# Columns beside the keys: zeros by a bf16 matmul, filled by GpSimd in SBUF from the fourth pair of heads on

## The chip, the cores and the metric

The kernel runs on one core of a Trainium2 chip. The metric is device microseconds of one execution. TensorE is PE in the rows (its weight loads PEld), VectorE is DVE, ScalarE is ACT, GpSimd is POOL, and SP is the queue that issues most of the DMAs.

## What is computed

Chunked attention with memory keys feeds a top-1 mixture of experts. The change lies in the attention, which is, cut to what matters:

```
B, H, S, D = 4, 8, 768, 64;  chunk, left, right, n_mem = 32, 16, 8, 8
for c in range(S // chunk):
    ctx = [max(0, 32*c - 16), min(S, 32*c + 40))
    k_full = concat(mem_k, k[ctx]);  v_full = concat(mem_v, v[ctx])
    scores = q[chunk c] @ k_full.T / sqrt(D)
    a = softmax(scores)                  # with the row's maximum taken off
    out[chunk c] = a @ v_full
x = out as [3072, 512];  e = argmax(x @ w_gate + bias);  y = gate * relu(x @ w1[e]) @ w2[e]
```

Chunk 0 has no 16 keys to its left, and chunk 23 no 8 keys to its right.

## The kernel before

The 32 heads are worked in 16 pairs, u = 0 to 15, and each pair in two halves of 12 chunks (hf = 0 and 1). I write S0(u) and S1(u) for the scores of the two halves. Every chunk has 64 key columns in the tile `kbd` (two buffers, by u % 2): 56 keys of the sequence and 8 memory keys. The two heads of a pair stand in the two halves of the partitions.

- `trans_k(u+1)` (L337), in the first half of pair u, transposes the keys of each head on PE into one PSUM bank (three transposes, L343). The bank has 8 columns to the left and 8 to the right of the keys, which the windows of chunks 0 and 23 reach into. A matmul in float32 fills these 16 columns with memory keys (L347), so that they never raise a row's maximum; the rows of V that belong to them are zero.
- `store_k` (L349) copies the windows from PSUM to `kbd`, four copies on ACT (L353).
- `mem_keys(u+2)` (L332) writes the 8 memory columns of every chunk, two copies on POOL (L335), one pair ahead.
- `share_v(u+1)` (L304), eight copies on POOL (L311), repeats the 24 rows of V that two chunks share. The first waits for V to land from DRAM. In the second half of pair u it stands on POOL ahead of `mem_keys(u+2)`, and behind both comes the store of the outputs of an earlier pair (L418).
- `exps_t` transposes scores (L379) and takes the exponential on ACT (L381, tile PT); `attend` multiplies by V (L391); `trans_x` transposes the output (L413), ACT copies it (L416).
- `route(b)` finds the experts of a batch of four pairs. Its steps are dealt out among those of the attention by `pump`. Where two of its one-hot pairs go to POOL (L663, L665), they stand behind L606 and L418 and ahead of the next `share_v`: this is so ahead of pairs 8, 12 and 15.

PE, SP and POOL run in the order in which the program is written, ACT and DVE too until pair 13. In the loop below, an iteration is one half of a pair: scores, exponentials of the half before, then in the first half `trans_k`, `store_k`, in the second `share_v`, `mem_keys`, `trans_q`, then `attend` of the half before.

Of the kernel before, what the change touches and what calls it, by code (L numbers as in the profile page):

```python
# [20 lines left out]
P = 128  # L21
B, H, S, D = 4, 8, 768, 64
NMEM = 8
NCH = S // 32
# [7 lines left out]
NTAIL = 8  # L32
NEXTRA = 7
HEAD = 3
LAST = 3
ROW_R1 = HEAD + NTAIL + 1
ROW_X = ROW_R1 + 1
# [15 lines left out]
def tile_chunk_attention_top1_moe(  # L53
# [14 lines left out]
    nc = tc.nc  # L68
# [24 lines left out]
    def bank():  # L93
        return ps.tile([P, 512], F32, name="tr", tag="tr", bufs=4)
# [14 lines left out]
    idle = const.tile([P, 640], BF16, name="idle")  # L109
# [16 lines left out]
    kbds = [pers.tile([P, NCH, 2, 64], F32, name=f"kbd{i}") for i in range(2)]  # L126
# [12 lines left out]
    mkp = pers.tile([P, P], F32, name="mkp")  # L139
# [9 lines left out]
    ident = const.tile([P, P], F32, name="ident")  # L149
# [19 lines left out]
    memT = pers.tile([P, 16, NMEM], F32, name="memT")  # L169
# [15 lines left out]
    listed, turn0, ends, tail_no, at_r1, at_x = (rows[:, i:i + 1] for i in range(6))  # L185
# [15 lines left out]
    def more_constants():  # L201
# [30 lines left out]
        yield "v"  # L232
        nc.vector.tensor_scalar(tail_no, row, HEAD - 0.5, None, op0=ALU.is_gt)
        yield "v"
# [3 lines left out]
        yield "v"  # L238
        nc.vector.scalar_tensor_tensor(turn0, turn0, float(HEAD - ROW_X), row, op0=ALU.mult, op1=ALU.add)
        yield "v"  # L240
        nc.vector.scalar_tensor_tensor(turn0, ends, float(ROW_X - HEAD + 2 - ROW_L - LAST), turn0, op0=ALU.mult, op1=ALU.add)
        yield "v"
        nc.vector.tensor_scalar(turn0, turn0, -2.0, None, op0=ALU.add)
        yield "v"
        nc.vector.tensor_scalar(tail_no, row, HEAD + NTAIL + 0.5, float(1 - 64), op0=ALU.is_gt, op1=ALU.mult)
        yield "v"
        nc.vector.tensor_add(tail_no, tail_no, row)
        yield "v"
        nc.vector.tensor_scalar(tail_no, tail_no, float(-HEAD), None, op0=ALU.add)
        yield "v"  # L250
# [53 lines left out]
    def share_v(u):  # L304

        vw = vws[u % NVW]
        for h in range(2):
            r0 = 64 * h
            for c in range(0, NCH - 1, 6):
                w = min(6, NCH - 1 - c)  # L310
                nc.gpsimd.tensor_copy(vw[r0:r0 + 24, h, c + 1:c + 1 + w, 0:D], vw[r0 + 32:r0 + 56, h, c:c + w, 0:D])  # L311

    def regroup_q(u):
        q2 = q2s.pop(u)
        qr = qrs[u] = wk.tile([P, 6, 2, D], F32, name="qr", bufs=1)
        nc.vector.tensor_copy(
            qr.rearrange("p x h d -> p h x d"), q2.rearrange("p h (x d) -> p h x d", d=D)
        )
# [18 lines left out]
    def trans_k(u):  # L337
        k2 = k2s.pop(u)
        for h in (1, 0):
            hh = 2 * u + h  # L340
            t = kts[u, h] = bank()
            for i in range(3):
                nc.tensor.transpose(t[:, 8 + i:8 + i + 382:3], k2[:, h, i * P:(i + 1) * P], ident)  # L343

            pads = bass.AP(tensor=t.tensor, offset=t.offset, ap=[list(t.ap[0]), [392, 2], [1, 8]])
            mem_sel = ident[:, 4 * hh:4 * hh + 4].unsqueeze(1).unsqueeze(1)
            nc.tensor.matmul(pads, mkp, mem_sel.to_broadcast([P, 2, 2, 4]), start=True, stop=True)  # L347

    def store_k(u, h, j, copy):  # L349
        tt = kts[u, h][64 * j:64 * j + 64]  # L350
        win = bass.AP(tensor=tt.tensor, offset=tt.offset, ap=[list(tt.ap[0]), [16, NCH], [1, 28]])
        dst = kbds[u % 2][64 * h:64 * h + 64, :, h, 0:56]
        copy(dst.rearrange("p c (i j) -> p c i j", j=2)[:, :, :, j], win)  # L353

    def scores(u, hf):
        kbd, qT = kbds[u % 2], qTs[u]
        sc = scs[u, hf] = ps.tile([P, 512], F32, name="sc", tag="sc", bufs=2)
        for t in range(3):
            for j in range(4):
                c = 4 * (3 * hf + t) + j  # L360
                nc.tensor.matmul(  # L361
                    sc[32 * j:32 * j + 32, t * P:(t + 1) * P], qT[:, 32 * c:32 * c + 32],
                    kbd[:, c].rearrange("p h m -> p (h m)"), start=True, stop=True,
                )

    def less_max(u, hf):
        scf = scs.pop((u, hf))[:, 0:384].rearrange("p (a m) -> p a m", m=64)
        mx = sm.tile([P, 6, 1], F32, name="mx")
        nc.vector.reduce_max(mx, scf, axis=AX.X)
        pump(1)  # L370
        sb = sbs[u, hf] = wk.tile([P, 6, 64], F32, name="sb")
        nc.vector.tensor_sub(sb, scf, mx.to_broadcast([P, 6, 64]))

    def exps_t(u, hf):

        sb = sbs.pop((u, hf)).rearrange("p a m -> p (a m)")
        t = bank()
        for i in range(3):
            nc.tensor.transpose(t[:, i * P:(i + 1) * P], sb[:, i * P:(i + 1) * P], ident)  # L379
        PT = PTs[u, hf] = wk.tile([P, 3 * P], F32, name="PT")  # L380
        nc.scalar.activation(PT, t[:, 0:384], AF.Exp, scale=scale)  # L381
# [82 lines left out]
    def plan_rest():  # L464
# [39 lines left out]
        vec.tensor_scalar(turn, ends, end[:, E - 1:E], turn0, op0=ALU.mult, op1=ALU.add)  # L504
        vec.tensor_scalar(nsl[:, 0:1], end[0:1, E - 1:E], float(2 - HEAD - LAST), None, op0=ALU.add)
        vec.tensor_mul(sta, sta, noth)
# [373 lines left out]
    nc.gpsimd.memset(vws[1][64:P, 0], 0.0)  # L880
    edge_v(1)
    trans_k(0)
    t = bank()
    nc.tensor.transpose(t[:, 0:P], mk, ident)
# [22 lines left out]
    for i in range(n + 2):  # L907
        live = i < n
        u, hf = units[i] if live else (NU, i % 2)
        now[0] = i  # L910
        if i == MAN:
            man.close()
        if live and i < n - 1:
            scores(u, hf)
        if 1 <= i <= n:
            exps_t(*units[i - 1])
        if live:
            less_max(u, hf)
            pump(1)
        if u + 1 < NU and hf == 0:  # L920
            trans_k(u + 1)
            regroup_q(u + 1)
            pump(3)
            store_k(u + 1, 1, 0, nc.scalar.copy)
            store_k(u + 1, 0, 0, nc.scalar.copy)
            store_k(u + 1, 0, 1, nc.scalar.copy)
            store_k(u + 1, 1, 1, nc.scalar.copy)
            pump(3)
        elif u + 1 < NU:
            share_v(u + 1)  # L930
            if u + 2 < NU:
                mem_keys(u + 2, nc.gpsimd)
            trans_q(u + 1)
            store_q(u + 1, 0)
            store_q(u + 1, 1)
            pump(5)
        elif live:
            pump(5)
        first = i in (n - 3, n - 2)
        if first:  # L940
            trans_x(*units[i - 2])
        if i == n - 2:
            scores(*units[i + 1])
        if 1 <= i <= n:
            attend(*units[i - 1])
        if i == n:
            trans_x(*units[i - 2])
            trans(0)
            trans(1)
            conv(4)  # L950
            conv(5, nc.gpsimd)
            normalize(*units[i - 1])
            mm1(0)
        if i > n:
            mm1(1)
        if i >= 2 and not first and i != n:
            trans_x(*units[i - 2])
        if 1 <= i < n:
            normalize(*units[i - 1])
            pump(1)  # L960
        if i >= 2:
            u2, hf2 = units[i - 2]
            if hf2 == 1 and u2 % 4 == 3:
                routing.append((route(u2 // 4), True, u2 // 4, 0))
        if i == 1:
            routing.append((more_constants(), False, -1, 0))
        if i == 6:
            assert not routing
            bias_rows()
        if i < n:  # L970
            pump(1, True)
        if live and hf == 0:
            if u + 3 < NU:
                load_qk(u + 3)
            if u >= 1 and u - 1 + NVW < NU:
                load_v(u - 1 + NVW)
        if (u, hf) == (NU - 2, 1):
            while routing:
                pump(99, True)
            c_ld.close()  # L980
            xp = ctx.enter_context(tc.tile_pool(name="xp", bufs=1, side="right"))
            ix = xp.tile([P, 2], I32, name="ix")
            gx = xp.tile([P, 2], I32, name="gx")
            xg = [xp.tile([P, XW], F32, name=f"xg{t}") for t in range(2)]
            xth, xtl = [xp.tile([P, 4, 256 + NR], F32R, name=f"xt{i}") for i in range(2)]
            hh, hl = [xp.tile([P, 8, 256], F32R, name=f"h{i}") for i in range(2)]
            load_w(0, 0)
            gather(0)
        elif u == NU - 1:
            conv(2 * hf)  # L990
            conv(2 * hf + 1, nc.gpsimd)
# [137 lines left out]
    more.close()  # L1129
    for i in range(1, LAST + 1):  # L1130
        slot(ROW_L + i if i < LAST else None)

# [29 lines left out]
```

## Time and profile before

| what | value |
|---|---|
| three runs | 442.55, 445.7, 446.6 us, median 445.7 |
| the profiled execution | 444.6 us, span 442.8 us |
| mean granted clock of TensorE in it | 0.989 of full speed |
| attention | about the first 137 us of the span |
| busy share PE / DVE / ACT / POOL | 94 / 70 / 61 / 46 % |

A row of the timeline gives the start and the length in us, the engine, the line of the kernel, the operation with its tiles and shapes, and in brackets how long the engine had waited and for whom. Rows of the same kind that follow each other on an engine are merged (x4 is four of them); the length then runs from the first start to the last end.

### The profile page before, as it was taken

To read this page: it belongs to the slowest core of one execution; us is meant where nothing else is said; L and a number is where in the kernel's file an instruction comes from. 1 tells how busy PE (TensorE), PEld (TensorE's weight loads), DVE (VectorE), ACT (ScalarE), POOL (GpSimd) and SP (SyncE) were. 2 spreads that over 40 slices of the span, in tenths; PEclk is the share of its full clock that TensorE was granted. 3 is DMA by queue.
4 is the path that set the end of the run, shared out by engine and by line. 5 is a ranking of instruction groups with operands and counts; after the bars stand their busy time and mean duration, and the time that the engine had idled before them with its cause. 6 is when DMAs were issued, how large, how long until landed. Compare 5 with 4: busy or idle time off the path is not lost. (4 is left out here: it accounts for less than half of the span.)

```text
span 442.8 us, 11872 instructions
## 1 busy us (share of the span) xinstructions
PE 418.2 (94%) x4053; PEld 355.5 (80%) x4053; DVE 308.2 (70%) x756; ACT 269.7 (61%) x537; POOL 203.9 (46%) x397
## 2 busy tenths in 40 slices
PE   6889999999987998999999999999999999999993
PEld 3757777777765887989898898989898988898982
DVE  8788598688787699657646366676868584959530
ACT  5767878777656663556456455666656565757521
POOL 8977779689798732651053305405031215220101
PEclk9999999999997999999999999999999999999998
DMA  7899999999988401277186977505596404340101
GB/s 205 143 210 224 226 222 222 203 226 203 217 196 261 147 1 51 95 215 224 52 234 197 228 213 242 190 6 170 125 246 220 139 5 146 97 143 2 47 1 47
DMA packets 73059, 69.10 MB, mean 156 GB/s; under 512 B 31275, under 2 KB 59139, under 8 KB 72980
## 3 DMA queue, kind: packets, MB, share of 16 engines
q1 hardware_dynamic: 65968, 48.86, 44.7%
q0 software_dynamic: 5888, 19.11, 14.5%
q8 instruction: 37, 0.61, 0.6%
q14 instruction: 42, 0.34, 0.3%
q10 hardware_dynamic: 1124, 0.18, 0.2%
HBM read 79.69 MB, written 16.43 MB: 217 GB/s over the span
## 5 line engine op out<-in xcount | busy, mean ns | idle before, releaser
L813 PEld LDWEIGHTS tr<-xt,w 128*128 128x128 f32 x1152 | 142.5, 190 | 5.0 <-issue 2.1
L813 PE MATMUL tr<-xt,w 128*128 128x256 f32 (+1 forms) x1152 | 144.7, 286 | 1.7 <-PEq L1123 0.6
L823 PE MATMUL av<-wh,h 128*128 128x512 f32 x384 | 124.9, 397 | 0.0
L817 DVE SCALAR_TENSOR_TENSOR h<-tr,h 128x256 fp32r<-128x256 f32 x96 | 40.5, 422 | 67.6 <-ACT h L814 41.3
L823 PEld LDWEIGHTS av<-wh,h 128*128 128x128 f32 x384 | 72.2, 188 | 16.6 <-issue 0.4
L823 PE MATMUL av<-wl,h 128*128 128x512 f32 x192 | 75.8, 395 | 0.0
L814 ACT ACTIVATE h<-tr 128x256 fp32r<-128x256 f32 x96 | 36.8, 384 | 56.0 <-PE tr L813 45.3
L311 POOL COPY vw<-vw 24x384 f32<-24x384 f32 (+1 forms) x128 | 61.1, 515 | 20.3 <-DMA vw<-in_v_dram 18.9
L848 POOL DMA_INDIRECT out_dram<-o,ix x24 | 24.7, 1028 | 93.9 <-ACT o L844 90.8
L738 DVE TENSOR_TENSOR wl<-raw,wh 128x512 fp32r<-128x512 f32 x91 | 62.8, 691 | 7.1
L738 DVE TENSOR_TENSOR w<-raw,w 128x512 fp32r<-128x512 f32 x93 | 60.6, 690 | 5.1 <-ACT w L736 2.5
L736 ACT CAST wh<-raw 128x512 fp32r<-128x512 f32 x96 | 58.8, 615 | 0.0
L736 ACT CAST w<-raw 128x512 fp32r<-128x512 f32 x96 | 52.9, 621 | 0.0
L353 ACT COPY kbd<-tr 64x672 f32<-64x672 f32 x62 | 48.4, 781 | 5.8 <-PE tr L347 4.7
L823 PEld LDWEIGHTS av<-wl,h 128*128 128x128 f32 x192 | 36.1, 188 | 7.7
L844 ACT ACTIVATE o<-av,gate 128x512 f32<-128x512 f32 x24 | 16.2, 689 | 39.0 <-PE av L823 30.7
L756 POOL DMA_INDIRECT xg<-xd,gx x24 | 26.8, 1117 | 16.6 <-POOL gx L754 5.4
L391 PE MATMUL av<-vw,PT 128*32 128x130 f32 x768 | 28.5, 277 | 4.4 <-ACT PT L381 3.1
L361 PE MATMUL sc<-kbd,qT 128*32 128x128 f32 x768 | 27.5, 276 | 2.7 <-POOL kbd L335 2.7
L381 ACT ACTIVATE PT<-tr 128x384 f32<-128x384 f32 x32 | 15.8, 494 | 17.6 <-PE tr L379 17.5
L391 PEld LDWEIGHTS av<-vw,PT 128*32 128x32 f32 x768 | 19.6, 108 | 8.6 <-ACT PT L381 6.0
L361 PEld LDWEIGHTS sc<-kbd,qT 128*32 128x32 f32 x768 | 19.3, 109 | 8.0 <-issue 3.8
(250 smaller groups left out, 511.3 us busy)
## 6 DMA issues: line engine op xcount, KB each, us to landing
raw<-in_moe_w_dram SPq DMA_DIRECT2D x192, 256.0 KB
k<-in_k_dram SPq DMA_DIRECT2D x16, 384.0 KB
q<-in_q_dram SPq DMA_DIRECT2D x16, 384.0 KB
xd<-xb POOLq DMA_DIRECT2D x16, 384.0 KB, 6.1
vw<-in_v_dram SPq DMA_DIRECT2D x32, 184.0 KB
xs<-xg SPq DMA_DIRECT2D x14, 256.0 KB
xq<-xs SPq DMA_DIRECT2D x28, 128.0 KB
vw<-spread_v SPq DMA_DIRECT2D x30, 48.8 KB
```

The lines of the kernel that those rows point to most:

```text
L311: nc.gpsimd.tensor_copy(vw[r0:r0 + 24, h, c + 1:c + 1 + w, 0:D], vw[r0 + 32:r0 + 56, h, c:c + w, 0:D])
L353: copy(dst.rearrange("p c (i j) -> p c i j", j=2)[:, :, :, j], win)
L361: nc.tensor.matmul(sc[32 * j:32 * j + 32, t * P:(t + 1) * P], qT[:, 32 * c:32 * c + 32], kbd[:, c].rearrange("p h m -> p (h m)"), start=Tr ...
L391: nc.tensor.matmul(avb[32 * j:32 * j + 32, t * W:(t + 1) * W], PT[:, t * P + 32 * j:t * P + 32 * j + 32], vw[:, :, c], start=True, stop=True,)
L736: nc.scalar.copy(wh[i], raw[i])
L738: (eng or nc.vector).tensor_sub(wl[i][:, s], raw[i][:, s], wh[i][:, s].bitcast(F32))
L756: nc.gpsimd.indirect_dma_start(out=xg[t], out_offset=None, in_=xd[0:rows], in_offset=bass.IndirectOffsetOnAxis(ap=gx[:, t:t + 1], axis=0))
L813: nc.tensor.matmul(pw, wt[i][:, j * P:(j + 1) * P], x[:, c, 0:w], start=(n == 0), stop=(n == 11))
L814: nc.scalar.activation(hh[:, f], ph, AF.Relu)
L817: nc.vector.scalar_tensor_tensor(hl[:, f], ph, 0.0, hh[:, f].bitcast(F32), op0=ALU.max, op1=ALU.subtract)
L823: nc.tensor.matmul(pos[t], x, w[8 + f], start=(f == 0 and n == 0), stop=(f == 7 and n == 2))
L848: nc.gpsimd.indirect_dma_start(out=out, out_offset=bass.IndirectOffsetOnAxis(ap=to[:, t:t + 1], axis=0), in_=outs[t], in_offset=None, boun ...
```

## The change

From pair 3 on, the float32 matmul with the memory keys is replaced by a bf16 matmul of zeros (the tile `idle`, which is there already), so the columns beside the keys come out as zero. The memory keys are then written over them in `kbd` by a new function, `edge_keys`: two small copies on POOL, one for each head (64 partitions, 2 x 16 columns), in the second half of the pair before, ahead of `share_v`.

```
+UEDGE = 3
...
             pads = bass.AP(tensor=t.tensor, offset=t.offset, ap=[list(t.ap[0]), [392, 2], [1, 8]])
-            mem_sel = ident[:, 4 * hh:4 * hh + 4].unsqueeze(1).unsqueeze(1)
-            nc.tensor.matmul(pads, mkp, mem_sel.to_broadcast([P, 2, 2, 4]), start=True, stop=True)
+            if u < UEDGE:
+                mem_sel = ident[:, 4 * hh:4 * hh + 4].unsqueeze(1).unsqueeze(1)
+                nc.tensor.matmul(pads, mkp, mem_sel.to_broadcast([P, 2, 2, 4]), start=True, stop=True)
+            else:
+                nc.tensor.matmul(pads, idle[:, 0:P], idle[:, 0:16].rearrange("p (a m) -> p a m", a=2), start=True, stop=True)
...
+    def edge_keys(u):
+        for h in range(2):
+            r = slice(64 * h, 64 * h + 64)
+            t = kbds[u % 2][r, 0, h]
+            ends = bass.AP(tensor=t.tensor, offset=t.offset, ap=[list(t.ap[0]), [P * (NCH - 1) + 48, 2], [NMEM, 2], [1, NMEM]])
+            nc.gpsimd.tensor_copy(ends, memT[r, u:u + 1, :].unsqueeze(1).to_broadcast([64, 2, 2, NMEM]))
...
         elif u + 1 < NU:
+            if u + 1 >= UEDGE:
+                edge_keys(u + 1)
             share_v(u + 1)
```

POOL, ahead of pair 8, before. The names: `kbd_125` is the buffer of the keys of pair 8, `vw_129` holds its V; the waits are on other engines' counters.

```order
L335 COPY kbd_125<-memT 64x24x8 [waits Pool_49]
L606 DMA xd<-gt 128x6x4 [waits DVE_49]
L418 DMA xd<-xb 128x6x128
L663 TENSOR_SCALAR l_1350<-iota,lo 128x128 [waits DVE_49,Pool_49]
L665 TENSOR_SCALAR a_1351<-iota,ac,tokm 128x192 [waits DVE_49]
L663 TENSOR_SCALAR l_1375<-iota,lo 128x128
L665 TENSOR_SCALAR a_1376<-iota,ac,tokm 128x192
L311 COPY vw_129<-vw_129 24x6x64 [waits DMAHW3_49,Pool_49]
```

The same place on POOL in the changed kernel, whose lines are numbered up to 11 higher here.

```order
L336 COPY kbd_125<-memT 64x24x8 [waits Pool_49]
L617 DMA xd<-gt 128x6x4 [waits DVE_49]
L429 DMA xd<-xb 128x6x128
L674 TENSOR_SCALAR l_1360<-iota,lo 128x128 [waits DVE_49,Pool_49]
L676 TENSOR_SCALAR a_1361<-iota,ac,tokm 128x192 [waits DVE_49]
L674 TENSOR_SCALAR l_1385<-iota,lo 128x128
L676 TENSOR_SCALAR a_1386<-iota,ac,tokm 128x192
L364 COPY kbd_125<-memT 64x2x16 [waits Activation_49]
L364 COPY kbd_125<-memT 64x2x16 [waits Activation_49,Pool_49]
L312 COPY vw_129<-vw_129 24x6x64 [waits DMAHW3_49,Pool_49]
```

The two copies of the edge keys (L364) are new between the one-hot pairs of the routing and the copies of V. They wait for the copies on ACT, and nothing else has moved.

PE at the scores S0(8) and the transposes of the keys of pair 9 that follow, before.

```order
L361 MATMUL sc<-kbd_125,qT 32x128 [waits Activation_49,Pool_49]
L361 MATMUL sc<-kbd_125,qT 32x128 x11
L379 MATMUL tr<-ident,sb 128x128 [waits DVE_49,PE_49]
L379 MATMUL tr<-ident,sb 128x128 x2
L343 MATMUL tr<-ident,k_923 128x128 [waits DMAHW5_49,PE_49]
L343 MATMUL tr<-ident,k_923 128x128 x2
L347 MATMUL tr<-ident,mkp 128x2x8
L343 MATMUL tr<-ident,k_923 128x128 [waits PE_49]
L343 MATMUL tr<-ident,k_923 128x128 x2
L347 MATMUL tr<-ident,mkp 128x2x8
```

The same place on PE in the changed kernel.

```order
L372 MATMUL sc<-kbd_125,qT 32x128 [waits Activation_49,Pool_49]
L372 MATMUL sc<-kbd_125,qT 32x128 x11
L390 MATMUL tr<-ident,sb 128x128 [waits DVE_49,PE_49]
L390 MATMUL tr<-ident,sb 128x128 x2
L344 MATMUL tr<-ident,k_927 128x128 [waits DMAHW5_49,PE_49]
L344 MATMUL tr<-ident,k_927 128x128 x2
L351 LDWEIGHTS idle
L351 MATMUL tr<-idle 128x2x8
L344 MATMUL tr<-ident,k_927 128x128 [waits PE_49]
L344 MATMUL tr<-ident,k_927 128x128 x2
L351 LDWEIGHTS idle
L351 MATMUL tr<-idle 128x2x8
```

Each float32 matmul (L347) has become a bf16 weight load and matmul (L351). The scores wait for POOL in both; before it was for the memory columns written a pair earlier, now it is for the edge copies shown above. From pair 5 on, one of the four copies on ACT also waits for the edge copies of two pairs before, which wrote the same buffer. DVE's and SP's orders are the same.

## Rows read from the trace of the kernel before

**Rows 1.** The page, busy time of PE over the whole span:

```profile
PE 418.2 (94%) x4053; PEld 355.5 (80%) x4053; DVE 308.2 (70%) x756; ACT 269.7 (61%) x537; POOL 203.9 (46%) x397
```

**Rows 2.** Timeline of pair 6, PE and ACT, from its first exponentials to S0(7):

```profile
58.72 0.30 PEld L347 LDWEIGHTS tr<-ident,mkp 128*128 128x128 f32 x2
58.76 0.49 ACT L381 ACTIVATE PT<-tr 128x384 f32<-128x384 f32 x1 [0.58 <-PE tr L379]
...
59.27 3.17 ACT L353 COPY kbd<-tr 64x672 f32<-64x672 f32 x4
...
62.46 0.48 ACT L416 COPY xT<-tr 128x384 f32<-128x384 f32 x1
...
62.84 0.50 ACT L381 ACTIVATE PT<-tr 128x384 f32<-128x384 f32 x1
...
63.47 0.60 PEld L391 LDWEIGHTS av<-vw,PT 128*32 128x32 f32 x24 [0.17 <-ACT PT L381]
...
64.75 0.86 PE L361 MATMUL sc<-kbd,qT 128*32 128x128 f32 x24
```

**Rows 3.** What ACT waited for before L353 (us, times), and one of these in the timeline:

```profile
  PE tr L347: 4.7, 3
...
27.67 3.17 ACT L353 COPY kbd<-tr 64x672 f32<-64x672 f32 x4 [0.25 <-PE tr L347]
```

**Rows 4.** Timeline, weight loads of six small bf16 matmuls:

```profile
60.74 0.23 PEld L592 LDWEIGHTS <-ones_b 128*128 128x128 bf16 x6
```

**Rows 5.** Timeline ahead of S0(8), POOL, one copy on DVE, PE:

```profile
63.82 3.65 POOL L311 COPY vw<-vw 24x384 f32<-24x384 f32 x8 [0.85 <-DMA vw<-in_v_dram]
...
67.07 0.82 DVE L316 COPY qr<-q 128x768 f32<-128x768 f32 x1
...
67.53 0.95 POOL L335 COPY kbd<-memT 64x192 f32<-64x192 f32 x2
...
72.12 0.86 PE L361 MATMUL sc<-kbd,qT 128*32 128x128 f32 x24
...
72.51 1.02 POOL L665 TENSOR_SCALAR a<-iota,ac,tokm 128x192 fp32r<-128x192 f32 x1
```

**Rows 6.** Timeline ahead of S0(12), POOL and PE:

```profile
95.95 4.02 POOL L311 COPY vw<-vw 24x384 f32<-24x384 f32 x8 [1.82 <-DMA vw<-in_v_dram]
...
103.11 0.86 PE L361 MATMUL sc<-kbd,qT 128*32 128x128 f32 x24
...
104.64 1.21 POOL L665 TENSOR_SCALAR a<-iota,ac,tokm 128x192 fp32r<-128x192 f32 x1
```

**Rows 7.** Copies on POOL (ns min/median/max; timeline), and scores that waited for one:

```profile
L335 POOL COPY kbd<-memT x32: 337/341/555, 10.0 to 123.8; 64x192 f32<-64x192 f32 x32
...
156.88 0.19 POOL L744 COPY ix<-ix 128x2 int32<-128x2 int32 x1
...
25.49 0.59 PEld L361 LDWEIGHTS sc<-kbd,qT 128*32 128x32 f32 x24 [0.57 <-POOL kbd L335]
```

**Rows 8.** Timeline ahead of S0(4), the last POOL instruction and the scores:

```profile
39.17 0.86 POOL L418 DMA_DIRECT2D xd<-xb  x1
...
41.22 0.86 PE L361 MATMUL sc<-kbd,qT 128*32 128x128 f32 x24
```

**Rows 9.** Timeline, SP's first request for the V of pair 11, and PE's last reading of that buffer's old V:

```profile
83.09 0.87 PE L391 MATMUL av<-vw,PT 128*32 128x130 f32 x24
...
89.54 1.63 SPq L295 DMA_DIRECT2D vw<-in_v_dram  x1
```

**Rows 10.** Timeline ahead of S0(15), the last one-hot of DVE, and the matmuls that take them:

```profile
128.88 0.40 DVE L665 TENSOR_SCALAR a<-iota,ac,tokm 128x192 fp32r<-128x192 f32 x1
...
129.22 0.63 PEld L673 LDWEIGHTS tr<-a,l 128*128 128x128 f32 x5 [1.52 <-POOL a L665]
```

**Rows 11.** Stretches: length, then busy (instructions) of PE, PEld, DVE, ACT, POOL, clock, DMA share, GB/s:

```profile
128.00:129.00 1.00, 0.00 (x0) 0.00 (x0) 1.00 (x5) 0.00 (x0) 1.00 (x2) 1.00 0.86 172
...
140.00:145.00 5.00, 4.80 (x21) 4.20 (x21) 3.23 (x6) 2.73 (x5) 4.15 (x9) 0.50 0.96 311
```

## Prediction

> **What bounds the kernel now.** I read the page first, then the timeline of the attention, then the timeline of POOL alone. On the page PE is busy for 94% of the span [rows 1], and from that one would pay for every matmul taken off it. The share is a mean, though, and in the attention a busy PE is not what sets the pace. The timeline of one pair shows it [rows 2]. In the first half of pair 6 the exponentials run on ACT until 59.25. ACT then makes the four copies of the keys (59.27 to 62.44), the copy of an earlier output (from 62.46) and the exponentials of the next half (62.84 to 63.34). `attend` starts 0.13 us behind these, at 63.47, and S0(7) follows at 64.75. After S0(7) come transposes and the exponentials of the next first half, and the ring closes. One turn takes 7.4 us (S0(7) at 64.75, S0(8) at 72.12 [rows 2, 5]). The float32 matmul beside the keys (PEld L347 at 58.72) lies in the first half on PE, while ACT goes from the exponentials straight into the copies: they start 0.02 us behind. PE has its slack in this stretch. The timelines of pairs 3 to 14 look the same at this place; I show one.
>
> Two things are to be seen on POOL. It works without a gap from the moment that V lands (0.85 us of waiting ended at 63.82) to the last one-hot of the routing, which ends at 73.53, while S0(8) has started at 72.12 [rows 5]. The same holds ahead of S0(12): V at 95.95, the last one-hot done at 105.85, S0(12) at 103.11 [rows 6]. So in these two places POOL is behind PE, and that costs nothing as long as PE needs nothing from its end.
>
> **What is taken away.** 26 float32 matmuls go (two for each of 13 pairs). Their two weight loads take 0.30 us on PE [rows 2]. Six bf16 weight loads with their matmuls are through in 0.23 us [rows 4], so I take 0.10 us, on the dear side, for a bf16 load and matmul: at most 0.20 us is saved each time, 5.2 us in all if PE were the bound. What counts is who waits for it. ACT's copies of the keys waited for L347 three times, 4.7 us in all [rows 3]. Of these the one at 27.67 is for pair 3 and can give its 0.25 us; the other two belong to pairs that keep the old form. For the other pairs the ring of [rows 2] hides the saving. I take 0.2 us.
>
> **What is added.** Two copies of 64 x 32 elements on POOL per pair. No such copy is in the trace. From below, a copy of 128 x 2 takes 0.19 us; from above, one of 64 x 192 takes 0.34 us in the median and 0.55 at most [rows 7], and a pair of them took 0.95 [rows 5]. 32 columns are nearest to the small one, so I take 0.21 us each and 0.5 us for the pair with its gaps; the range keeps 0.4 and 0.95.
>
> The Trainium skill, SBUF — State Buffer, section "Who interferes with whom", says that a GpSimd instruction blocks for the whole of a VectorE instruction that holds the port pair which both share, a plain copy among them. The trace agrees: the pair of copies of 0.95 us stands beside a DVE copy that ran from 67.07 to 67.89 [rows 5]. By that rule the two edge copies would take up to the 0.95 us that I keep as the upper end; by the median of the rows alone, 0.5 us.
>
> **The waits.** The first edge copy waits for the four ACT copies. Behind it on POOL stand `share_v`, `mem_keys`, the output's store and the next one-hots; S0 of the pair waits for the second. ACT's copies are done at 62.44 for S0(7) at 64.75 [rows 2], 2.3 us ahead, so this wait alone is covered. What isn't covered is where POOL is late:
> - Eleven of the thirteen pairs: POOL has finished what stands ahead before S0 is due. The smallest such margin while nothing has shifted is at pair 4: POOL free at 40.03, S0(4) at 41.22, that is 1.19 us [rows 8]. An edge pair of 0.5 us fits, and one of 0.95 too. V isn't late by it, since POOL waits for V there. I cost these at nothing.
> - S0(8): POOL free at 73.53. With 0.5 us for the edge pair and 0.05 us to PE (the scores that waited for an L335 copy started that soon, [rows 7]) the scores start at 74.1 instead of 72.12. That is 2.0 us.
> - S0(12): 105.85 + 0.55 = 106.4, instead of 103.11. That is 3.3 us from the old times. The question is whether the 2.0 us from before are in it or come on top. POOL's stretch begins when V of pair 11 lands. SP asked for that V from 89.54 on; PE had read the old V of that buffer by 83.96 [rows 9]. So 5.6 us lay between, SP was held by its own transfers and not by PE, and a PE that is 2.0 us later doesn't move them. V lands where it did, POOL's stretch stays in place, and 2.0 us of the 3.3 us are there already: 1.3 us more.
> - S0(15): the matmuls that collect the one-hots waited 1.52 us for POOL until 129.22, but DVE's last one-hot ends at 129.28 [rows 10], and DVE's routing goes with PE. With PE and DVE 3.3 us late POOL no longer decides; what is given back is how far the five matmuls had been strung out behind POOL and not DVE, 0.35 us. POOL's edge pair for pair 15 is ready by then.
> - The extra wait of ACT's copies from pair 5 on is for edge copies two pairs old, some 14 us earlier (two turns of the ring): nothing. The weight loads that are now separate instructions hide beside the transposes' matmuls.
>
> **The sum.** -0.2 + 2.0 + 1.3 - 0.35 = +2.75 us. After S0(15) everything hangs on what came before it (the first expert's weights are asked for when the third batch's routing is done), so I carry it to the end undiminished. On the profiled execution that gives 444.6 + 2.75 = 447.35; the median of the runs shown is 1.1 us higher and would give 448.45. I take 447.9, between them. A measurement of this kernel tells a change of about 1% from none: under 441.2 or over 450.2.
>
> **The rivals.**
> - *The two stalls add up.* If V of pair 11 comes later with PE, POOL's stretch moves and S0(12) loses its whole 3.3 us: -0.2 + 2.0 + 3.3 - 0.35 = +4.75, so 449.9; with the edge pairs at 0.95 us, 0.45 more at each place, 450.8. For it: SP takes V only in turn with K and Q, and some of these wait for PE. Against it: the 5.6 us of [rows 9]. It decides once PE is more than 5.6 us late there, or SP's queue is that much faster. This ends above 1%, about.
> - *The clock falls in the stall.* At S0(8) PE would have nothing to do for 2.0 us. Against it: one whole microsecond without a matmul, in a wait of 1.52 us, left the granted clock at full speed [rows 10, 11]. For it: it went to half, the 1.2 GHz level, shortly after several waits, and stayed there for the five microseconds shown [rows 11]. Such a stretch of 5 us does 2.5 us of work less. That takes 447.9 to 450.4, and 452.9 if it happens at both stalls.
> - *POOL is in time.* If V lands 2 to 3 us earlier in relation to PE than in this execution, the stretches ahead of S0(8) and S0(12) end early enough and nothing changes: 444.4 to 445.5. Against it: both are late, by 1.4 and 2.7 us.
> - *PE is the bound after all.* Then the 5.2 us come, less what of the stalls remains: 440 without them, 443 with 2.75 us of them. Against it: `attend` hangs on the exponentials by 0.13 us [rows 2].
>
> **How the numbers follow.** Forecast (446 to 449.7) 0.50; stalls add up (449.5 to 451) 0.20; clock 0.10; POOL in time 0.13; PE the bound 0.07. The predicted time is the first's. The range from 444.4 to 451.2 leaves out most of the last case and the upper half of the clock's, about 1 in 10, and part of the ends of the others. Slower by over 1%: half of the second case, most of the third, and 0.08 of the first through the scatter of the runs: 0.28. Faster by over 1%: the PE case without stalls, 0.05. Within 1%: 0.67.
>
> **What would show it.** In the changed trace the scores S0(8) and S0(12) wait for the edge copies on POOL, about 2 us and 1.5 us, and no other S0 waits over 0.5 us. V of pair 11 lands near 96. ACT's copies keep their 3.2 us and their place right behind the exponentials, and the distance from S0(6) to S0(7) stays at 7.4 us although PE's first half is shorter. The forecast is wrong if S0(8) doesn't wait, if V moves with PE, if the turn of the ring gets shorter, or if the clock is at half inside the attention.

## The result, and the profile after

| | before | after |
|---|---|---|
| median of 20 runs each, us | 445.72 | 448.58 |
| range of these, us | 442.55 to 449.85 | 445.8 to 452.62 |
| profiled execution, us (span) | 444.6 (442.8) | 448.84 (447.0) |
| mean granted clock in it | 0.989 | 0.985 |

The ratio after to before is 1.0064, with a 95% interval of 1.0042 to 1.0086; the longest run of the changed kernel, 452.62 us, counts as a slow one and is not in it. By the ratio the change makes the kernel slower by 2.85 us, which is within 1%, where 67 of 100 chances had been put. The steps summed to +2.75 us. The total agrees better than its parts do: the two stalls came where they were forecast but cost 0.9 us each and not 2.0 and 1.3, and a third long turn, which was not forecast, came on top.

The page of the changed kernel answers to [rows 1]. PE has 26 instructions fewer and the same busy time (418.2 before), and POOL has 26 more and 8.8 us more, of which the new copies, at 0.21 us in the median, make about 5.5:

```profile
PE 418.9 (94%) x4027; PEld 352.2 (79%) x4027; DVE 308.0 (69%) x756; ACT 269.3 (60%) x537; POOL 212.7 (48%) x423
```

The new instructions, from the groups by line (ns min/median/max, then first and last start in us). The bf16 load is three times cheaper than the two float32 loads of [rows 2], and an edge copy takes 0.21 us:

```profile
L351 PEld LDWEIGHTS <-idle x26: 97/98/98, 28.6 to 125.1; 128*128 128x128 bf16 x26
...
L364 POOL COPY kbd<-memT x26: 201/209/388, 31.5 to 130.4; 64x32 f32<-64x32 f32 x26
```

The waits of the changed kernel between 30 and 135 us of the span (us in total, times, longest):

```profile
POOL kbd L364 <- ACT kbd L357: 8.4, 11, 1.5
...
POOL vw L312 <- DMA vw<-in_v_dram: 3.8, 4, 1.5
...
PEld sc L372 <- POOL kbd L364: 2.1, 2, 1.1
```

And one row of the same view of the kernel before:

```profile
POOL vw L311 <- DMA vw<-in_v_dram: 18.9, 10, 3.8
```

Two things are to be seen. Exactly two scores wait for edge copies, 2.1 us together. And POOL's waits have changed their owner: before, POOL waited for V to land (18.9 us), and now mostly for ACT's copies of the keys (8.4 us), because the edge copies stand in front of `share_v`.

The timeline ahead of S0(8) in the changed kernel (weight loads of the scores, POOL) answers to [rows 5]:

```profile
62.98 0.21 POOL L364 COPY kbd<-memT 64x32 f32<-64x32 f32 x1 [0.58 <-ACT kbd L357]
63.25 3.68 POOL L312 COPY vw<-vw 24x384 f32<-24x384 f32 x8
...
65.16 0.59 PEld L372 LDWEIGHTS sc<-kbd,qT 128*32 128x32 f32 x24 [0.17 <-POOL vw L312]
...
71.97 1.02 POOL L676 TENSOR_SCALAR a<-iota,ac,tokm 128x192 fp32r<-128x192 f32 x1
72.93 0.47 POOL L364 COPY kbd<-memT 64x32 f32<-64x32 f32 x2
...
73.45 0.59 PEld L372 LDWEIGHTS sc<-kbd,qT 128*32 128x32 f32 x24 [1.07 <-POOL kbd L364]
```

S0(7) is at 65.16, POOL works without a gap from 62.98 to the end of the edge pair at 73.40, and S0(8) starts 0.05 us behind it. The same ahead of S0(12), which answers to [rows 6]:

```profile
95.17 3.68 POOL L312 COPY vw<-vw 24x384 f32<-24x384 f32 x8
...
97.09 0.59 PEld L372 LDWEIGHTS sc<-kbd,qT 128*32 128x32 f32 x24 [0.17 <-POOL vw L312]
...
104.84 0.47 POOL L364 COPY kbd<-memT 64x32 f32<-64x32 f32 x2
...
105.36 0.59 PEld L372 LDWEIGHTS sc<-kbd,qT 128*32 128x32 f32 x24 [1.07 <-POOL kbd L364]
```

The starts of the scores give the best ruler for this kernel, because they are far sharper than a run's total. Here is the time from one S0 to the next, in us, taken from the starts of the scores' weight loads in the profiled executions. I use it for all kernels below:

| kernel | 3 to 4 | 6 to 7 | 7 to 8 | 8 to 9 | 11 to 12 | 13 to 14 | 14 to 15 | S0(3) to S0(15) |
|---|---|---|---|---|---|---|---|---|
| before | 7.36 | 7.43 | 7.37 | 8.44 | 7.38 | 8.58 | 9.79 | 96.11 |
| before, once more (e12) | 7.36 | 7.43 | 7.37 | 8.45 | 7.39 | 8.57 | 11.54 | 98.79 |
| changed | 7.37 | 7.43 | **8.29** | 8.48 | **8.27** | **9.54** | 9.65 | 98.71 |
| changed, once more (e8) | 7.37 | 7.41 | **8.26** | 8.49 | **8.25** | **9.40** | 9.61 | 98.45 |

Three turns are longer, each by about 0.9 us, and all other turns up to S0(14) are the same within 0.1 us. One exception warns of the limits: the second execution of the kernel before has 11.54 us where the first has 9.79, and 9.45 us from S0(12) to S0(13) where the first has 8.48. In both places PE waited for POOL's one-hots, with no edge copy in the kernel. Ahead of that S0(13) POOL had begun to copy V of pair 11 only 1.75 us behind S0(11), where the first execution has 0.23, and was late by it (a row of the second):

```profile
106.89 0.63 PEld L673 LDWEIGHTS tr<-a,l 128*128 128x128 f32 x5 [0.95 <-POOL a L665]
```

So the end of the attention scatters by more than the whole effect, and a total up to S0(15) or to the end of the span from one execution decides nothing. Ratios of runs stand beside it for that.

### The profile page after: what moved, and what is told of

Its sections match the earlier page's. It is cut to its first block, busy times and chain, and to the rows that moved or that the text cites. A ratio compares the mean times of both kernels' runs of the same rounds, so it can differ in the third digit from the quotient of the medians.

```text
span 447.0 us, 11882 instructions
## 1 busy us (share of the span) xinstructions
PE 418.9 (94%) x4027; PEld 352.2 (79%) x4027; DVE 308.0 (69%) x756; ACT 269.3 (60%) x537; POOL 212.7 (48%) x423
## 5 line engine op out<-in xcount | busy, mean ns | idle before, releaser
L824 PEld LDWEIGHTS tr<-xt,w 128*128 128x128 f32 x1152 | 140.9, 188 | 4.7 <-issue 2.4
L824 PE MATMUL tr<-xt,w 128*128 128x256 f32 (+1 forms) x1152 | 142.9, 284 | 1.6 <-PEq L1142 0.5
L767 POOL DMA_INDIRECT xg<-xd,gx x24 | 25.9, 1078 | 16.1 <-POOL gx L765 5.2
L372 PE MATMUL sc<-kbd,qT 128*32 128x128 f32 x768 | 29.1, 287 | 3.8 <-POOL kbd L336 2.2
L380 DVE TENSOR_REDUCE mx<-sc 128x6 f32<-128x384 f32 x32 | 17.7, 554 | 14.9 <-PE sc L372 12.4
```

Of the source, the lines that this page charges most:

```text
L372: nc.tensor.matmul(sc[32 * j:32 * j + 32, t * P:(t + 1) * P], qT[:, 32 * c:32 * c + 32], kbd[:, c].rearrange("p h m -> p (h m)"), start=Tr ...
L767: nc.gpsimd.indirect_dma_start(out=xg[t], out_offset=None, in_=xd[0:rows], in_offset=bass.IndirectOffsetOnAxis(ap=gx[:, t:t + 1], axis=0))
L824: nc.tensor.matmul(pw, wt[i][:, j * P:(j + 1) * P], x[:, c, 0:w], start=(n == 0), stop=(n == 11))
```

## The experiments

The theory before the first of them: ACT's ring sets the pace, so the bf16 zeros bring nothing, and the cost is PE's waiting at S0(8) and S0(12) for edge copies that stand behind POOL's one-hots. The rivals: the zeros bring something and the copies cost more elsewhere; the copies themselves cost, in all 13 pairs.

**e1, the zeros alone.** The edge copies are left out, so this kernel doesn't put the memory keys into the columns beside the keys (they stay zero).

```
-            if u + 1 >= UEDGE:
-                edge_keys(u + 1)
```

> The bf16 zeros from pair 3 on, without the edge copies on POOL: the columns beside the keys stay zero. This is the PE part of the change alone. Theory (the ring over ACT sets the pace of the attention): 0.2 us less than the kernel before, within 1 us of it. Rival (PE is the bound and the change as made hides its gain behind the stalls): up to 5.2 us less.

**e2, the copies alone.** All pairs keep the float32 matmul, and the edge copies write the same values over it.

```
-            if u < UEDGE:
+            if True:
```

> The float32 matmul stays for all pairs and the edge copies on POOL are added from pair 3 on. Theory: the copies carry all of the cost, so as slow as the changed kernel, 2.9 us over the kernel before, with S0(8) and S0(12) waiting for the edge copies. Rival (the bf16 matmul saves PE time that the copies eat up): slower than the changed kernel by what it saves.

**e3, all but the two places**: pairs 8 and 12 keep the old form and have no edge copies. **e4, the two places alone**: only these have the new one.

```
-            if u < UEDGE:
+            if not (u >= UEDGE and u not in (8, 12)):     # e3
+            if not (u in (8, 12)):                        # e4
...
-            if u + 1 >= UEDGE:
+            if u + 1 >= UEDGE and u + 1 not in (8, 12):   # e3
+            if u + 1 in (8, 12):                          # e4
```

> The change in all its pairs but 8 and 12, which keep the float32 matmul and get no edge copies. Theory (the cost is the two waits behind the routing's one-hots, and what these push PE into later): within 0.7 us of the kernel before. Rival (each pair pays, through POOL's time or collisions with DVE): eleven thirteenths of the cost, 2.4 us over the kernel before.

> The change in pairs 8 and 12 alone. Theory: all of the cost, 2 to 3 us over the kernel before. Rival (each pair pays): two thirteenths, 0.4 us over it.

What the four gave (e9 and e10 are the kernels of e2 and e4 once more):

| kernel | ratio to before | 95% interval | 7 to 8 | 11 to 12 | 13 to 14 | scores that waited for an edge copy |
|---|---|---|---|---|---|---|
| e1 | 1.0008 | 0.9984 to 1.0033 | 7.35 | 7.39 | 8.56 | none |
| e2 | 1.0018 | 0.9991 to 1.0044 | 9.71 | 8.75 | 9.48 | S0(8) 2.50, S0(12) 1.54 |
| e9 (as e2) | 1.0034 | 1.0010 to 1.0058 | 9.73 | 8.24 | 9.39 | S0(4) 0.34, S0(8) 2.53, S0(12) 1.04 |
| e3 | 1.0026 | 0.9999 to 1.0053 | 7.39 | 7.37 | 8.29 | S0(13) 0.63 |
| e4 | 1.0013 | 0.9989 to 1.0038 | 8.46 | 8.89 | 9.60 | S0(8) 1.24, S0(12) 1.68 |
| e10 (as e4) | 1.0014 | 0.9984 to 1.0044 | 8.70 | 8.68 | 9.08 | S0(8) 1.49, S0(12) 1.45 |

The first reading is sure, since it stands in every execution. Without the copies there is no long turn (e1), with the copies at pairs 8 and 12 alone there are all three (e4, e10), and with them everywhere else there is none of the three (e3, where S0(12) to S0(13) took 8.93 us instead of 8.48). The zeros change no turn of the ring: e1's 7.34, 8.32, 7.76 and 7.42 us from S0(3) to S0(7) are the 7.36, 8.35, 7.76 and 7.43 of before.

The second reading is not sure. The ratios of the parts are too close to 1 to be told apart: e3, where only S0(13) waits, has the larger ratio of the two (+1.2 us, with 1.2 to either side), and e4 with all three long turns +0.6 us, with 1.1 to either side. The single profiled executions don't help: S0(3) to S0(15) took 96.96 us in e3 and 99.93 in e4, 3.0 us apart, and the ratios stand the other way round. One thing the intervals do say: e4's ends at 1.7 us, and that of the whole change begins at 1.9. So in the timed runs the stalls at pairs 8 and 12 hardly account for the whole cost, though e10's interval reaches 2.0.

Beside what was expected, e1 went as the theory had it (+0.4 us, with 1.1 to either side, and not -5.2). e2 did not: 0.8 us where 2.9 was expected. Nor did e4: 0.6 us where 2 to 3 were expected, which is nearer to its rival's 0.4. e3's 1.2 us lies between its theory's 0.7 and its rival's 2.4.

**How long a stall is.** The executions with a stall show a rule that the prediction's sum already had in it. From the first copy of V on POOL to the end of the edge pair the same work stands in a row, so the wait of S0 follows from when that first copy starts beside the S0 before it. "Start" is its distance to S0(7) or S0(11):

| execution, place | start | what POOL waited for | wait of the next S0 | wait less start |
|---|---|---|---|---|
| changed, S0(8) | -1.91 | ACT's copies | 1.07 | 2.98 |
| changed, S0(12) | -1.92 | ACT's copies | 1.07 | 2.99 |
| e4, S0(8) | -1.70 | V, 1.66 us | 1.24 | 2.94 |
| e10, S0(8) | -1.52 | V, 1.50 us | 1.49 | 3.01 |
| e10, S0(12) | -1.49 | V, 0.69 us | 1.45 | 2.94 |
| e4, S0(12) | -1.26 | V, 2.08 us | 1.68 | 2.94 |
| e9, S0(8) | -0.46 | V, 1.30 us | 2.53 | 2.99 |
| e2, S0(8) | -0.67 | V, 0.58 us | 2.50 | 3.17 |

So the wait is 3 us plus the start, within 0.06 us in all of these but the last, where POOL waited another 0.29 us for V between the copies. The four places that are left out (both of e8, S0(12) of e2 and of e9) give 2.95 or 2.96. (And the turn grows by 0.15 us less than the wait, since S0's weight loads stand idle for 0.17 us ahead of S0 in other turns too, as at 65.16: 1.07 and 0.92 in the changed kernel, 1.49 and 1.33 in e10.) In the kernel before, V's copies began at 63.82 with S0(7) at 64.75 [rows 2, 5], a start of -0.93, which gives a wait of 2.0 us, as the prediction had it. In the changed kernel they began at -1.91, right behind the edge copies, which is the earliest that ACT's copies allow. The start scatters from one execution to the next: up to the V of pair 7 e12, e4 and e10 run the same program as the kernel before, and they have -0.90, -1.70 and -1.52.

**e9 and e10** are the same kernels as e2 and e4, and **e12** is the kernel before, to see which of these numbers come again.

> The float32 matmul for all pairs with the edge copies from pair 3 on, once more. Theory (the copies carry the cost of the change): 2 to 3 us over the kernel before, as the changed kernel. Rival (the bf16 zeros have a part in it, or the first measurement of 0.8 us stands): within 1.2 us of it. In the trace S0(8) and S0(12) are 0.9 us late or more; if V of pair 7 lands after the four copies on ACT the wait is longer by that much.

> The change in pairs 8 and 12 alone, once more. Theory (two waits of 0.9 us or more, and what they push PE into): 1.5 to 3 us over the kernel before. Rival (the end of the attention gives it back): within 0.8 us of it.

> The kernel before, a second look. If V lands where its transfers put it and not where PE is, the starts of POOL's copies of V against S0 of the same pair differ by a microsecond or so from the first look, while the turns of the ring are equal within 0.05 us.

The stalls came again in their places, and the small ratios came again too. e9's 1.5 us (0.4 to 2.6) is less than the 2 to 3 that its theory had and more than its rival's 1.2; e10's 0.6 us is what its rival had, that the end of the attention gives the delay back. e12 is the row "before, once more" of the first table. Its turns agree with those of before within 0.05 us up to S0(12), as expected. Its start at S0(8) is -0.90 where before has -0.93, no scatter at all, and at S0(12) it is 1.75 where before has 0.23, more than the microsecond that was expected.

**The clock behind a stall.** In e2 and e9 not only the turn to S0(8) is long but the next one too: 9.83 and 9.82 us where all others have 8.4 to 8.5 (8.6 and 8.8 in e5 and e6, further down, whose turns are all longer). The granted clock tells why. Stretches of e2 (columns as in [rows 11]); S0(8) starts at 74.13:

```profile
74.13 1.05 PEld L372 LDWEIGHTS sc<-kbd,qT 128*32 128x32 f32 x24 [2.50 <-POOL kbd L364]
```

```profile
70.00:73.00 3.00, 1.52 (x29) 0.91 (x27) 2.75 (x7) 1.78 (x5) 2.91 (x5) 1.00 0.98 179
74.00:75.00 1.00, 0.87 (x19) 0.81 (x23) 0.00 (x0) 0.00 (x0) 0.94 (x3) 0.50 0.94 221
75.00:76.00 1.00, 1.00 (x14) 0.62 (x7) 0.29 (x1) 0.00 (x0) 0.94 (x4) 0.50 1.02 338
76.00:77.00 1.00, 1.00 (x8) 1.00 (x7) 0.96 (x3) 0.43 (x1) 1.00 (x3) 0.50 1.38 198
77.00:78.00 1.00, 1.00 (x16) 0.97 (x19) 0.34 (x1) 0.62 (x2) 1.00 (x2) 0.90 1.32 118
```

After the wait of 2.50 us PE came back at half clock, the 1.2 GHz level. It stayed there for three whole microseconds (0.50 from 74 to 77) and the start of a fourth, and the scores took 1.05 instead of 0.59 us to load. The same happened behind the wait of 1.54 us in e2 (clock 0.50 from 108 to 111 us) and behind the 2.53 us in e9 (0.57 in the mean from 74 to 78). The stretches of the changed kernel, where both waits were 1.07 us:

```profile
73.00:74.00 1.00, 0.55 (x20) 0.55 (x24) 0.20 (x1) 0.14 (x1) 0.89 (x4) 1.00 0.96 236
74.00:76.00 2.00, 2.00 (x43) 1.68 (x39) 1.58 (x3) 1.08 (x2) 1.94 (x5) 1.00 1.12 268
...
106.00:110.00 4.00, 4.00 (x77) 3.31 (x68) 3.07 (x7) 3.13 (x5) 3.83 (x9) 1.00 1.14 153
```

There the clock stayed at full speed. It did so too behind 1.24 and 1.68 us in e4 and 1.49 and 1.45 us in e10, so the length of the wait alone doesn't decide it.

**e8 and e7, the whole change, and the change without its stalls.** e8 is the changed kernel as it is. e7 has the same instructions, but the one-hots that the first two batches give to POOL are held back until the edge copies are issued. The one-hots lose their place, not the copies.

```
+            if b < 2 and eng is nc.gpsimd:
+                held.append(one_hot)
...
             if u + 1 >= UEDGE:
                 edge_keys(u + 1)
+            while held:
+                held.pop(0)()
             share_v(u + 1)
```

> The changed kernel as it is, once more, beside the three that follow. If its cost is the same everywhere it is again 2.9 us (1.9 to 3.8) over the kernel before, clearly more than the parts of it measured so far (the copies alone 0.8, pairs 8 and 12 alone 0.6, all but these 1.2, each give or take 1.1). If the first comparison overstated it, about 1 us. In the trace S0(8) and S0(12) wait for the edge copies.

> The changed kernel with POOL's one-hots of the first two batches put behind the edge copies of pairs 8 and 12, so that these copies don't stand behind 3.3 us of routing. Theory (the waits of S0(8) and S0(12) are the cost): neither S0 waits over 0.3 us, time within 1 us of the kernel before and 2 us under the changed kernel. Rival (POOL's extra work or its collisions with DVE are the cost): as slow as the changed kernel.

e8 gave 1.0069 (1.0040 to 1.0099), e7 1.0030 (1.0000 to 1.0059) beside the same runs of the kernel before. POOL in e7:

```profile
72.46 0.21 POOL L364 COPY kbd<-memT 64x32 f32<-64x32 f32 x1 [0.53 <-ACT kbd L357]
72.78 0.62 POOL L676 TENSOR_SCALAR l<-iota,lo 128x128 fp32r<-128x128 f32 x1
73.40 1.02 POOL L677 TENSOR_SCALAR a<-iota,ac,tokm 128x192 fp32r<-128x192 f32 x1
74.39 0.61 POOL L676 TENSOR_SCALAR l<-iota,lo 128x128 fp32r<-128x128 f32 x1
74.97 1.02 POOL L677 TENSOR_SCALAR a<-iota,ac,tokm 128x192 fp32r<-128x192 f32 x1
```

and its S0(8), which is not late for it:

```profile
74.56 0.59 PEld L372 LDWEIGHTS sc<-kbd,qT 128*32 128x32 f32 x24 [0.17 <-POOL a L677]
```

The edge pair is done at 72.67, 1.9 us ahead. The turns are 7.39, 7.39 and 8.70 us, those of before within 0.12, and S0(3) to S0(15) took 96.26 us: all three long turns are gone with the two waits. So the waits behind the one-hots cause them. By the ratios e7 is 1.3 us over the kernel before (0 to 2.6), where up to 1 was expected, and e8 3.1 us, as expected. That is 1.7 us between them, where 2 were expected: more than half of the cost goes with the waits, though the intervals of the two overlap, and e4 and e10, which have these waits, cost only 0.6. Where the rest of e7 comes from the traces don't show; it may be nothing, its interval begins at 1. Its profiled execution, 446.97 us, can't tell: the clock was at half in it ahead of S0(3), which came at 36.30 us and not at 33.15 to 34.62 as in all others.

```profile
29.00:33.00 4.00, 3.58 (x35) 2.74 (x35) 1.71 (x9) 2.61 (x4) 3.59 (x7) 0.57 1.11 268
```

**e5, e6 and e11, the ring.** e5 is the kernel before with one more float32 matmul on PE for each pair from pair 3 on. e6 is the changed kernel with the edge copies on ACT, behind the four copies of the keys, in the first half of the pair. e11 is the kernel before with one copy taken out of the ring: the copy of an earlier output, which stands between the copies of the keys and the next exponentials [rows 2], comes behind the exponentials.

```
+            for _ in range(2 if u >= 3 and h == 1 else 1):                      # e5, around L347
...
-            nc.gpsimd.tensor_copy(ends, memT[r, u:u + 1, :].unsqueeze(1).to_broadcast([64, 2, 2, NMEM]))
+            nc.scalar.copy(ends, memT[r, u:u + 1, :].unsqueeze(1).to_broadcast([64, 2, 2, NMEM]))     # e6
...
+        if later:                                                              # e11, in trans_x
+            put_off.append((xTs[u][:, 0:384], t[:, 0:384]))
+            return
```

> The kernel before with the float32 matmul beside the keys done twice for one head of each pair from 3 on: 13 more of them, 0.30 us each on PE. Theory (PE has 0.4 us of slack in each turn of the ring): no slower than 0.5 us over the kernel before, the distance from S0(6) to S0(7) stays at 7.4 us. Rival (PE is the bound): 3.9 us over it.

> The changed kernel with the edge copies on ACT, right behind the four copies of the keys, and not on POOL. Theory (ACT is in the ring): each turn is 0.4 to 0.6 us longer, 13 turns make 5 to 8 us over the kernel before, less what the end of the attention gives back. Rival (ACT is not in the ring): within 1 us of the kernel before, since POOL's waits are gone.

> The kernel before, with one copy moved on ACT: the copy of the earlier output of a pair's first half (L416) is put behind the exponentials of the next half and not ahead of them. All is computed. Theory (the ring runs over ACT's four copies, this copy of 0.48 us and the exponentials): each turn is up to 0.4 us shorter, bounded by PE, which has its own work done 0.1 to 0.4 us after that; 1 to 4 us under the kernel before. Rival (PE or a PSUM bank sets the turn): turns stay at 7.4 us, no gain.

| kernel | ratio to before | 95% interval | 3 to 4 | 4 to 5 | 5 to 6 | 6 to 7 | 11 to 12 |
|---|---|---|---|---|---|---|---|
| before (its profile) | | | 7.36 | 8.35 | 7.76 | 7.43 | 7.38 |
| e5, 0.3 us more on PE | 1.0032 | 1.0005 to 1.0059 | 7.43 | 8.46 | 7.89 | 7.51 | 7.52 |
| e6, 0.46 us more on ACT | 1.0110 | 1.0071 to 1.0149 | 7.79 | 8.75 | 8.09 | 7.79 | 7.79 |
| e11, 0.48 us less on ACT | 0.9978 | 0.9955 to 1.0001 | 7.01 | 7.97 | 7.86 | 7.45 | 7.01 |

ACT in e6: the pair of small copies stands between the copies of the keys and the copy of the output.

```profile
60.35 3.19 ACT L357 COPY kbd<-tr 64x672 f32<-64x672 f32 x4
...
63.56 0.46 ACT L364 COPY kbd<-memT 64x32 f32<-64x32 f32 x2
...
64.04 0.48 ACT L427 COPY xT<-tr 128x384 f32<-128x384 f32 x1
64.42 0.50 ACT L392 ACTIVATE PT<-tr 128x384 f32<-128x384 f32 x1
```

What is put on ACT there lengthens the turn almost at full price (0.33 to 0.43 us for 0.46), and what is taken off shortens it by 0.35 to 0.38 us for 0.48, in some turns and not in others. Work on PE comes through at 0.07 to 0.14 us for 0.3. So the ring over ACT holds the pace, but PE's slack beside it is not complete: e5 was expected to cost at most 0.5 us with turns as before; it cost 1.4 us (0.2 to 2.6), and its turns are longer. e6 cost 4.9 us (3.2 to 6.6), where 5 to 8 were expected. e11 is the one changed program with a median below that of before (445.68 against 446.81): 1.0 us less, where 1 to 4 were expected, and its interval just reaches 1.

**The third long turn.** No edge copy stands ahead of S0(14). The timeline of the kernel before at that place, DVE's routing of the third batch and POOL:

```profile
118.18 0.17 DVE L573 TENSOR_SCALAR eq<-l 128x48 f32<-128x48 f32 x1
...
118.85 0.19 DVE L575 TENSOR_TENSOR eq<-eq,rev 128x48 f32<-128x48 f32 x1
118.97 0.16 DVE L600 TENSOR_SCALAR sx<-sx 128x6 f32<-128x6 f32 x1
...
119.34 3.99 POOL L311 COPY vw<-vw 24x384 f32<-24x384 f32 x8 [2.53 <-DMA vw<-in_v_dram]
```

and of the changed kernel:

```profile
119.69 3.67 POOL L312 COPY vw<-vw 24x384 f32<-24x384 f32 x8
...
120.64 0.50 DVE L584 TENSOR_SCALAR eq<-l 128x48 f32<-128x48 f32 x1
...
121.62 0.49 DVE L586 TENSOR_TENSOR eq<-eq,rev 128x48 f32<-128x48 f32 x1
122.03 0.50 DVE L611 TENSOR_SCALAR sx<-sx 128x6 f32<-128x6 f32 x1
...
123.07 0.29 PE L603 MATMUL tr<-oh,ones_b 128*128 128x48 bf16 x6 [0.74 <-DVE oh L592]
```

Before, three small instructions of DVE ran just ahead of POOL's copies of V and took 0.16 to 0.19 us. After, PE and DVE are later by the two stalls while V is not, the same instructions fall beside the copies of V, and take 0.49 to 0.50 us. PE, which takes their result, waits 0.74 us. e5 shows that no edge copy is needed for this: it has none, it is 1.3 us late at S0(13) (79.0 us from S0(3), where before has 77.7), these instructions take 0.47, 0.48 and 0.50 us beside copies of V that began at 118.07, and its turn from S0(13) to S0(14) is 9.33 us.

```profile
118.07 3.72 POOL L311 COPY vw<-vw 24x384 f32<-24x384 f32 x8 [2.59 <-DMA vw<-in_v_dram]
...
119.10 0.47 DVE L574 TENSOR_SCALAR eq<-l 128x48 f32<-128x48 f32 x1
...
120.07 0.48 DVE L576 TENSOR_TENSOR eq<-eq,rev 128x48 f32<-128x48 f32 x1
120.47 0.50 DVE L601 TENSOR_SCALAR sx<-sx 128x6 f32<-128x6 f32 x1
...
121.50 0.29 PE L593 MATMUL tr<-oh,ones_b 128*128 128x48 bf16 x6 [0.52 <-DVE oh L582]
```

Nor is lateness alone enough. e12 was 0.9 us late at S0(13), but its copies of V began only at 121.60, behind these instructions (from 118.47, 0.16 to 0.20 us each), and its turn is 8.58 us. e6, later still, has its copies of V from 117.30 to 120.97 and these three instructions behind them, at 0.34, 0.19 and 0.16 us, and its turn is 8.51 us. In e7 V's copies begin between them, at 120.91: of the two that fall beside them one takes 0.47 us and the other 0.20. In e10 all three fall beside the copies, two take 0.42 and 0.48 us and the other 0.19, and its turn, 9.08 us, lies between the short and the long ones. So not every instruction beside a copy is slowed. I ran no kernel that moves V's copies alone, so the cause rests on executions that agree, not on its removal.

The Trainium skill, SBUF — State Buffer, section "Who interferes with whom", has VectorE and GpSimd share one port pair: where a VectorE instruction takes that pair too, whichever starts first holds it and the other waits. The prediction had used it in one direction only, DVE slowing POOL. The traces agree with it in the other: 0.16 to 0.20 us became 0.42 to 0.50 us. They show the lengths and not the port, and the two instructions that were not slowed (e7, e10) stay unexplained.

## Why the prediction was right, point by point

**The ring sets the pace, the shorter matmul brings nothing: right.** S0(6) to S0(7) is 7.43 us in both, as in e1, and e11 and e6 move it by work on ACT. The remark that PE has its slack there was too strong: e5's 0.3 us cost about 0.1 us a turn. The 0.2 us for pair 3 can't be seen, since S0(3) itself starts anywhere from 33.15 us (e1) to 34.62 (e8), and at 36.30 in e7. The price of the bf16 matmul was misread, though nothing hung on it: the 0.23 us of [rows 4] are the six weight loads alone, and here one load takes 0.10 us and its matmul 0.17.

**The edge pair takes 0.5 us: right.** 0.47 us, and 0.21 us each. Eleven of the thirteen pairs show no wait over 0.2 us, as forecast. But the margins are thinner than the 1.19 us that the prediction gave as the smallest. It looked only at the pairs ahead of the first stall; ahead of S0(13), at 111.59, POOL was free in the kernel before just 0.39 us early, less than an edge pair:

```profile
110.29 0.91 POOL L418 DMA_DIRECT2D xd<-xb  x1
```

In the changed kernel the two stalls have pushed PE back by then. In e3, which has no such stalls, S0(13) waits 0.63 us. And in e9 S0(4) waited 0.34 us.

**S0(8) waits, +2.0 us: right in place, sized too high.** The turn grew by 0.92 us and in e8 by 0.89. The step that failed is "POOL free at 73.53": the time at which V lands was taken over from one execution. SP's last request for that V began at 62.45 before, and in the changed execution at 61.26, 1.2 us earlier:

```profile
61.26 0.64 SPq L303 DMA_DIRECT2D vw<-spread_v  x1
```

while S0(7) was later by 0.4 us. With V there, POOL could start as early as ACT's copies let it, 1.91 us ahead of S0(7) instead of 0.93. The table of starts holds the measured price: 1.0 us at least, when POOL waits for ACT, and up to 2.5 us, when it waits for V.

**S0(12), +1.3 us, with the first stall contained in it: the size came near, the reason failed.** That V doesn't go with PE was right: SP asked for it from 89.20 on, 89.54 before [rows 9], although PE was 1.4 us later at S0(11), and POOL found it there at 95.17. But "POOL's stretch stays in place" doesn't follow any more. The edge copies stand ahead of V's copies and wait for ACT, and ACT goes with PE. So POOL's stretch moved with PE, its start was -1.92 us to S0(11) as it was -1.91 to S0(7), and the second stall came on top of the first, 0.89 us (0.87 in e8). That is the mechanism of the rival "the two stalls add up", with another cause than the one it named. Both together are 1.8 us, where 3.3 were forecast and 5.3 by the rival.

**Nothing else on the way: wrong.** The turn to S0(14) took 0.96 us more (0.82 in e8). The prediction looked at what the late PE waits for on POOL, and not at what DVE, late with it, meets on POOL.

**S0(15), -0.35 us: right in kind, the size is open.** The turn is shorter by 0.14 and 0.18 us against the first execution of before. The wait of [rows 10] for POOL's one-hots is gone, and DVE decides:

```profile
131.82 0.19 PEld L684 LDWEIGHTS tr<-a,l 128*128 128x128 f32 x1 [0.78 <-DVE a L676]
```

Given that this turn took 11.54 us in e12, such a size can't be called shown. The kind can: in the four executions without the three long turns and with the ring as it was (before, e12, e1 and e3) PE waits here for POOL's one-hots and the turn takes 9.79 to 11.54 us, and in the six with them (changed, e8, e2, e9, e4, e10) it waits for DVE's and the turn takes 9.61 to 10.14. So more may be given back here than 0.35 us.

**The sum.** Forecast -0.2 + 2.0 + 1.3 - 0.35 = +2.75. Measured in the traces, up to S0(15): 0.92 + 0.89 + 0.96 - 0.14 and what the other turns add, +2.6 us (98.71 against 96.11), in e8 +2.3; against e12's 98.79 it would be nothing. Timed: +2.85 and +3.1 us. So the total came out by luck, through two errors that go against each other: stalls too large by 1.5 us and 0.9 us forgotten.

**"Carried undiminished to the end": not shown.** The changed kernel agrees with it, but e2 and e9 were 7.3 and 5.8 us later at S0(15) and cost 0.8 and 1.5 us by their ratios, and e4 and e10 3.8 and 3.3 us later and cost 0.6. Either part of a delay is given back at the end of the attention, or the profiled executions are no fair sample of the timed ones. For e2 the second holds: the profiled one, 449.8 us, is the second longest of its 12 runs and 2.9 us over their median. What the timed cost of each part is stays open, and so does why the parts (e2 to e4) don't add up to the whole.

**The rivals.** *The clock falls in the stall* (0.10): it fell in e2 and e9, and cost 1.4 us in the next turn (9.83 instead of 8.44), not in the change itself. *POOL is in time* (0.13): half of it came true, V was earlier, but the edge copies' own wait for ACT sets a floor, and with the one-hots behind it POOL was still 1.07 us late. *PE is the bound*: excluded by e1. And that POOL's lateness "costs nothing as long as PE needs nothing from its end" in the kernel before holds for its first execution only: PE does need the one-hots, and in e12, with POOL later, it waited 0.95 us for them.

## What to carry to other kernels

An instruction put ahead of others in an engine's queue brings its own wait with it: ask what the whole stretch behind it waited for before (here V from DRAM) and what it waits for now (here ACT), because that decides whether a delay is absorbed or passed on. For a wait behind a fixed row of work, write it as a constant plus the start of that row (here 3.0 us less 0.5 to 1.9), and ask how that start scatters, not only what it was in one trace or in two that agree. When engines are made late by different amounts, look for pairs that slow each other and that had just missed each other before.

## What the runs showed of the hardware that was not expected

- Small DVE instructions (128x48 and 128x6 float32) mostly took 0.42 to 0.50 us beside POOL's copies from SBUF to SBUF, and 0.16 to 0.20 us ahead of them.
- A wait of PE of 2.5 us was followed by half clock both times, one of 1.54 us once, but 1.24, 1.45, 1.49 and 1.68 us were not.
- A copy of 64 x 32 elements took 0.21 us on POOL, and a pair of them 0.46 us on ACT, so this small work costs the same on both; where it stands decides.
- Two executions of the same kernel before differ by 2.7 us at S0(15) (96.11 and 98.79 us from S0(3)), although their turns up to S0(12) agree within 0.05 us.
